# Channel attention on one core: in its second pass the first packed group is unfolded only behind the raw rows and the first streamed rows

## The chip, the cores and the metric

The kernel runs on one core of one Trainium2 chip. The metric is the device time in microseconds (us) of one execution. The kernel before took 721.81 us, the median of three runs (721.34 to 722.48).

## The reference, cut to what matters

```python
# x: (1, 384, 384, 384) bfloat16, w1d: (1,) bfloat16, k = 1
g = jnp.einsum("bhwc->bc", x) / (H * W)
s = _sigmoid(g * w1d[0])          # the loop over k has one turn, the padding is empty
return x * s[:, None, None, :]
```

Every channel is averaged over all 147456 pixels, and then the whole of x is multiplied by one factor per channel. The factor is known only when the last pixel has been read, so x is needed twice: once for the sum and once for the product. In bfloat16 x has 113.2 MB. The on-chip arena of the kernel holds 275 "rows"; a row is 384 values in each of the 128 partitions, 96 KB in all, and x is 1152 rows.

## The kernel before, in words

**Pass one** loads all 1152 rows with DMAs that SP issues (L236, `load`), and TensorE adds each row to one PSUM accumulator (L242 and L256, `sum_rows`). Of the rows, 785 are *streamed*: they pass through the arena and are lost, so that pass two has to load them again. The other 367 are *kept*, in two ways. The 71 *raw* rows lie in the arena as they are. The others are kept as *groups*, in packed form: a group of 4q rows is folded into 3q rows by bit operations on VectorE (L276 `bits`, L282 `join`), since the bits of a quarter of the rows fit into unused bits of the other three quarters; ScalarE keeps a note of whether they did (L313). There are ten groups: group 0 (16 rows), groups 1 to 8 (32 rows each, four in each of two columns of the arena) and group 9 (24 rows, whose packed rows wait in PSUM banks). At the end of pass one ScalarE makes the factor (L443, a sigmoid).

**Pass two** multiplies all 1152 rows and stores them (`scale`, L456, nearly always on VectorE; `store`, L466, by SP), and loads the 785 streamed rows again into whatever rows of the arena have become free. A group is turned back into rows by `unfold`: for each of its two pieces (16 rows each) come the steps `fields` (four `bits` and two `join`), `three` (one `bits`, one `join`, a `scale` of 12 rows) and `fourth` (one `bits`, a `scale` of 4 rows). A group needs scratch rows (the 8 rows called Y), and its column needs 8 rows (U or V) that hold raw rows at first; `needed` says when these have been stored.

**What sets the order.** Nothing in pass two is ordered on the chip by choice. A planner in the kernel's Python code runs ahead of time with a clock of its own, `now`, in steps of 0.05 us, which begins at 0 when the factor is ready. It assumes a time for every step (`TS`, `TT`), for every row that a DMA moves (`ROW` 0.2267 us) and for the landing of a DMA, and writes the instructions into the queue of each engine in the order in which they come in this plan. On the chip each engine takes its queue strictly in order, and waits where its next instruction needs something that is not there (class `Flow`). SP's queue holds all loads and stores of pass two: a store that waits for VectorE holds back every load behind it. These rules of the planner matter here:

- When VectorE is free in the plan, the planner takes the next step of a group already begun; if there is none, it may begin a group (`start_group`), but only if nothing is left of three pieces that GpSimd scales at the start (`alongside`), and if either the DMA backlog is at least 24 us or no landed rows wait (`landed`).
- Landed rows are scaled first as long as the backlog of DMA work is under 24 us; else unfolding comes first.
- Streamed rows are loaded into the longest run of free rows, at once if the run is 32 rows or more, else only if the backlog has fallen under 9 us (8 rows or more) or under 4 us (any number).

The rows in which the work begins: the raw rows are stored first, in pieces of 4, 4, 4, 4, 8, 8, 13 and 13 rows by VectorE, and 4, 4 and 5 by GpSimd. Arena rows 220 to 232 and 233 to 245 are the two 13-row pieces, 246 to 258 the three pieces of GpSimd, 259 to 266 the piece called T. The first streamed loads of pass two go into these rows. In the plan of the kernel before, the first group (group 7) begins at 13.00, when the last 13-row piece has been scaled and the first streamed rows have not landed.

Of the kernel before, what the change touches and what calls it, by code (L numbers as in the profile page):

```python
# [127 lines left out]
def kernel(  # L128
# [45 lines left out]
    BANKED = len(GROUPS)  # L174
# [30 lines left out]
    def rows(lo, n):  # L205
        return [("a", r) for r in range(lo, lo + n)]
# [168 lines left out]
    def of_group(g):  # L375
        return [i for i, piece in enumerate(pieces) if piece[0] == g]
# [93 lines left out]
    def unfold(k, first):  # L470

        g, lo, p = pieces[k]
        a, at = first + 3 * lo, first + 3 * GROUPS[g][1] + lo
        w, wc = flat(a, 3 * p), [rows(a + j * p, p) for j in range(3)]
        w0, w1, w2 = (flat(a + j * p, p) for j in range(3))
        ba, ca = Y, Y + PIECE
        u, b, c = flat(at, p), flat(ba, p), flat(ca, p)
        uc, bc, cc = rows(at, p), rows(ba, p), rows(ca, p)

        def fields():  # L480
            bits(u, w0, SHR, 4, AND, 0x0780, wc[0], uc)
            bits(b, w1, SHR, 8, AND, 0x0078, wc[1], bc)
            bits(c, w2, SHR, 12, AND, 0x0007, wc[2], cc)
            join(u, u, b, OR, uc + bc, uc)
            bits(b, w2, SHL, 4, AND, 0x8000, wc[2], bc)
            join(u, u, c, OR, uc + cc, uc)

        def three():
            wall = wc[0] + wc[1] + wc[2]
            bits(w, w, AND, 0x87FF, OR, 0x3800, wall, wall)  # L490
            join(u, u, b, OR, uc + bc, uc)
            scale(a, 3 * p)

        def fourth():

            bits(u, u, XOR, FIX, AND, 0xFFFF, uc, uc)
            scale(at, p)

        return [
            (fields, 4 * TS(p) + 2 * TT(p)),  # L500
            (three, TS(3 * p) + TT(p) + TT(3 * p)),
            (fourth, TS(p) + TT(p)),
        ]
# [66 lines left out]
    now = dve_at = 0.0  # L570
# [5 lines left out]
    def release(a, n):  # L576
        for i in range(a, a + n):
            idle[i] = True
# [14 lines left out]
    def send(chunk, a, lo, hi, then, known=None):  # L593

        waiting.append((dve_at, hi - lo, then, chunk, a, lo, [] if known is None else known))
# [11 lines left out]
    needed = [set(SCRATCH + rows(U, 8)), set(SCRATCH + rows(V, 8)), set(SCRATCH)]  # L607
# [31 lines left out]
    free = [True, True, True]  # L639
# [3 lines left out]
    bank_at = None  # L643
# [4 lines left out]
    def start_group():  # L648

        if not line:  # L650
            return False
        g = line[0]
        column = home[g]
        if needed[column] or not free[column] or g == BANKED and (bank_at is None or now < bank_at[1]):
            return False
        line.popleft()
        free[column] = False
        a, q = GROUPS[g]
        if g == BANKED:
            a = bank_at[0]  # L660

        below = 0
        if column < 2 and g != COLUMNS[column][0]:
            below = GROUPS[COLUMNS[column][COLUMNS[column].index(g) - 1]][1]

        def part():
            release(a + below, sent - below)

        def done():
            nonlocal out_rows  # L670
            out_rows += 1
            free[column] = True
            release(a + max(below, sent), 4 * q - max(below, sent))

        for k in of_group(g):
            fields, three, fourth = unfold(k, a)
            turns.extend((fields + (None,), three + (None,), fourth + (None,)))
        sent = 0
        if len(line) >= total - N_SPLIT and q == PAIR:

            f, t, _ = turns[-5]
            sent = 3 * PIECE
            turns[-5] = (f, t, lambda: send(KEPT, a, c_group[g], c_group[g] + sent, part, written))
        f, t, _ = turns[-1]
        turns[-1] = (f, t, lambda: send(KEPT, a + sent, c_group[g] + sent, c_group[g] + 4 * q, done, written))
        return True

    while True:

        if dve_at <= now:  # L690
            ahead = backlog()
            can = bool(turns)
            if not can and not alongside and (ahead >= PENDING or not landed):
                can = start_group()
            if landed and (ahead < PENDING or not can):
                chunk, a, lo, n, end = landed.popleft()
                scale(a, n, s=s_ps if alongside and now else s_bf)
                dve_at = now + TT(n)
                since = (a, lo) if since is None else since
                if end or ahead < MERGE:  # L700
                    b, first = since
                    send(chunk, b, first, lo + n, stored(b, lo + n - first))
                    since = None
            elif can:
                f, t, then = turns.popleft()
                f()
                dve_at = now + t
                if then:
                    then()
# [18 lines left out]
        if bank_at is None and len(line) <= total - BANKS_AT and got and max(got)[0] >= PS * 4 // 3:  # L728
# [7 lines left out]
            bank_at = (a, now + 5.0)  # L736
# [59 lines left out]
```

## Time and profile before

| what | value |
|---|---|
| time, median of three runs | 721.81 us (721.34 to 722.48) |
| profiled execution, first to last instruction (span) | 719.6 us |
| VectorE (DVE) busy | 494.0 us, 69% |
| TensorE (PE) busy | 210.5 us, 29% |
| ScalarE (ACT) busy | 115.7 us, 16% |
| bytes moved by DMA | 303.79 MB, mean 422 GB/s |
| HBM read, written | 190.41 MB, 113.25 MB |
| last matmul done, factor begun | 268.3 us |

The page gives no other time for the profiled execution than its span; the median of the runs lies 2.2 us above that. In the profile, L12 is line 12 of the kernel; DVE is VectorE, and SPq is the queue of SP, which issues the DMAs. A row of the timeline gives the start, the duration, the engine, the line, the operation, out<-in and a count; what stands in brackets is idle time and what ended it. 128x1536 is 128 partitions by 1536 elements, that is 4 rows of 384. A row of the windows gives a stretch of the span and the busy time of every engine in it, and at its end the granted TensorE clock, the busy share of the DMA engines and the rate that they moved.

### The profile page before, as it was taken

What the parts mean: (1) busy time and instruction counts of PE and PEld (TensorE: products, weight loads), DVE (VectorE), ACT (ScalarE), POOL (GpSimd) and SP (SyncE); (2) the same over time, 40 slices, a digit from 0 to 9 for tenths busy, and PEclk for the clock granted to TensorE, in tenths of its full rate; (3) what the DMA queues carried; (4) which work ended last, traced back from release to release, by engine and by line L of the source; (5) the groups of instructions that cost most, each with busy time, mean ns of one, the idle gap of its engine ahead of it and who ended that gap; (6) DMA issues with size and microseconds to landing.
All of it is one profiled execution on the core that took longest, in us unless ns stands there. A gap on an engine that the chain in (4) does not pass through costs nothing.

```text
span 719.6 us, 2061 instructions
## 1 busy us (share of the span) xinstructions
PE 210.5 (29%) x1202; PEld 0.3 (0%) x3; DVE 494.0 (69%) x471; ACT 115.7 (16%) x93; POOL 10.6 (1%) x7
## 2 busy tenths in 40 slices
PE   4678689888887770000000000000000000000000
PEld 0000000000000000000000000000000000000000
DVE  4600004887999819988999998999998985095500
ACT  3600003665777610002000000000000000000000
POOL 0000000000000005000000000000000000000000
PEclk9999999999999995555555555555555555555555
DMA  9999999999999979999999999999999999999997
GB/s 381 431 441 428 426 430 432 438 434 429 422 427 427 429 324 369 422 394 423 429 432 437 426 431 445 427 428 439 432 427 442 427 436 430 437 435 426 437 438 318
DMA packets 20173, 303.79 MB, mean 422 GB/s; under 512 B 2242, under 2 KB 2242, under 8 KB 6082
## 3 DMA queue, kind: packets, MB, share of 16 engines
q1 hardware_dynamic: 20160, 303.67, 99.0%
q8 instruction: 4, 0.07, 0.0%
q14 instruction: 7, 0.06, 0.0%
q10 hardware_dynamic: 2, 0.00, 0.0%
HBM read 190.41 MB, written 113.25 MB: 422 GB/s over the span
## 4 chain that ended last, share of the span: by engine, by line
DMA 61%; DVE 21%; ACT 6%; PE 5%; another core or an unknown queue 1%; SPq 0%; issue 0%; DVEq 0%
DMA arena<-in_x_dram 40%; DMA out_dram<-arena 21%; DVE arena L456 14%; ACT arena L313 6%; PE bank L242 5%; DVE arena L276 5%; DVE arena L282 2%; SPq L236 0%; ACT s_bf L443 0%; SPq L791 0%; DVEq L112 0%; SPq L106 0%
## 5 line engine op out<-in xcount | busy, mean ns | idle before, releaser
L456 DVE TENSOR_TENSOR arena<-arena,s_bf 128x4608 bf16<-128x4608 bf16 (+8 forms) x97 | 228.8, 2390 | 68.2 <-DMA arena<-in_x_dram 52.3
L276 DVE TENSOR_SCALAR arena<-arena 128x1536 uint16<-128x1536 uint16 (+2 forms) x247 | 145.3, 633 | 111.8 <-DMA arena<-in_x_dram 102.0
L242 PE MATMUL bank<-arena,ones 128*128 128x384 bf16 x1151 | 202.1, 336 | 48.9 <-DMA arena<-in_x_dram 48.9
L313 ACT ACTIVATE arena<-arena 128x3072 uint16<-128x3072 uint16 (+1 forms) x38 | 102.4, 2696 | 142.3 <-DVE arena L276 142.3
L282 DVE TENSOR_TENSOR arena<-arena 128x1536 uint16<-128x1536 uint16 (+2 forms) x114 | 121.0, 1061 | 5.2 <-PE bank L242 2.7
L529 PE MATMUL bank<-odd,ones 128*128 128x1 bf16 x1 | 0.2, 188 | 322.7 <-DVE odd L524 322.7
L456 POOL TENSOR_TENSOR arena<-arena,s_bf 128x1536 bf16<-128x1536 bf16 (+1 forms) x3 | 10.4, 3484 | 268.9 <-ACT bank L447 268.9
L386 ACT COPY arena<-bank 128x512 uint32<-128x512 uint32 (+1 forms) x7 | 4.0, 571 | 58.4 <-DMA out_dram<-arena 58.2
L456 DVE TENSOR_TENSOR arena<-arena,bank 128x1536 bf16<-128x1536 bf16 (+2 forms) x7 | 11.3, 1688 | 0.0
L242 PE MATMUL bank<-zeros,ones 128*128 128x384 bf16 x48 | 8.3, 326 | 0.0
L313 ACT ACTIVATION_READ_ACCUMULATOR arena<-arena 128x1 f32 x38 | 7.1, 186 | 0.0
L386 ACT COPY bank<-arena 128x512 uint32<-128x512 uint32 (+1 forms) x7 | 3.6, 566 | 0.0
L443 ACT ACTIVATE s_bf<-bank,w_sc 128x384 bf16<-128x384 f32 x1 | 0.6, 581 | 14.5 <-PE bank L242 14.5
L256 PE MATMUL bank<-arena,ones 128*128 128x384 bf16 x1 | 0.5, 478 | 6.9 <-DMA arena<-in_x_dram 6.9
L764 ACT ACT_TABLE_LOAD x1 | 1.3, 1283 | 0.7 <-PEq L780 0.7
L343 DVE TENSOR_SCALAR w_sc<-bank 128x1 f32<-128x1 f32 x1 | 0.2, 159 | 1.1 <-PE bank L338 1.1
L333 DVE MEMSET ones<- 128x128 bf16 x1 | 0.2, 165 | 1.0 <-SPq L106 1.0
L338 PE MATMUL bank<-w_bf,ones 1*128 1x1 bf16 x1 | 0.2, 181 | 2.1 <-DMA w_bf<-in_w1d_dram 2.1
L529 PEld LDWEIGHTS bank<-odd,ones 128*128 128x128 bf16 x1 | 0.1, 106 | 581.7 <-DVE odd L524 581.7
L533 DVE CAST odd_i<-bank 128x1 int32<-128x1 f32 x1 | 0.2, 159 | 0.3 <-PE bank L529 0.3
L447 ACT COPY bank<-s_bf 128x192 uint32<-128x192 uint32 x1 | 0.3, 323 | 0.0
L519 DVE TENSOR_REDUCE worst<-seen 128x1 f32<-128x38 f32 x1 | 0.2, 184 | 0.0
(8 smaller groups left out, 0.9 us busy)
## 6 DMA issues: line engine op xcount, KB each, us to landing
arena<-in_x_dram SPq DMA_DIRECT2D x15, 4608.0 KB, 35.4
arena<-in_x_dram SPq DMA_DIRECT2D x21, 1248.0 KB, 13.5
out_dram<-arena SPq DMA_DIRECT2D x7, 3072.0 KB, 33.1
arena<-in_x_dram SPq DMA_DIRECT2D x6, 3072.0 KB, 26.5
out_dram<-arena SPq DMA_DIRECT2D x4, 4608.0 KB, 39.2
arena<-in_x_dram SPq DMA_DIRECT2D x6, 2304.0 KB, 18.2
arena<-in_x_dram SPq DMA_DIRECT2D x3, 4512.0 KB, 27.0
out_dram<-arena SPq DMA_DIRECT2D x10, 1248.0 KB, 12.0
```

The source lines that it names most:

```text
L242: return pe.add_instruction(mybir.InstMatmult(name=nc.get_next_instruction_name(), ins=[pe.lower_ap(rhs), pe.lower_ap(ones[:])], outs=[pe. ...
L256: return nc.tensor.matmul(acc, lhsT=ones[:], rhs=arena[:, i, :], start=first, stop=last)
L276: lambda: nc.vector.tensor_scalar(out=dst, in0=src, scalar1=s0, scalar2=s1, op0=op0, op1=op1),
L282: "DVE", lambda: nc.vector.tensor_tensor(out=dst, in0=a, in1=b, op=op), reads=reads, writes=writes
L313: lambda: nc.scalar.activation(out=y, in_=y, func=ACTF.Copy, accum_out=seen[:, 2 * k + i : 2 * k + i + 1]),
L333: fl.add("DVE", lambda: nc.vector.memset(ones[:], 1.0), writes=["ones"])
L386: "ACT", lambda: nc.scalar.copy(dst.bitcast(u32), src.bitcast(u32)), reads=reads, writes=writes
L443: lambda: nc.scalar.activation(out=s_bf[:], in_=acc, func=ACTF.Sigmoid, scale=w_sc[:, 0:1]),
L447: "ACT", lambda: nc.scalar.copy(s_ps.bitcast(u32), s_bf[:].bitcast(u32)), reads=["s_bf"], writes=["bank0"]
L456: lambda: vec.tensor_tensor(out=v, in0=v, in1=s[:, None, :].to_broadcast([P, n, C]), op=Op.mult),
L529: lambda: nc.tensor.matmul(votes, lhsT=ones[:], rhs=odd[:], start=True, stop=True),
L764: nc.scalar.preload_act_table(ACTF.Sigmoid)
```

## The change

One condition is added where a group may begin:

```diff
     def start_group():
         if not line:
             return False
         g = line[0]
         column = home[g]
-        if needed[column] or not free[column] or g == BANKED and (bank_at is None or now < bank_at[1]):
+        if now < 26.0 or needed[column] or not free[column] or g == BANKED and (bank_at is None or now < bank_at[1]):
             return False
```

Until its clock shows 26.0 the planner begins no group. The rest of the planner is as it was, so everything behind this point of the plan comes out differently as a consequence: what VectorE does between 13 and 26, which rows are free when, how large the loads are that go into them, and where the stores stand in SP's queue.

What comes out, in the clock of the plan: the first group begins at 27.25 instead of 13.00, the second at 64.40 instead of 44.30, the third at 100.40 instead of 79.30, and the last at 327.55 instead of 315.90. Up to the 13-row load into arena row 220 the queue of SP is the same in both. From the last raw store on it reads (number of rows, and in brackets the arena row where they begin):

```
before                                  after
store 13 (233), load 8 (246)            store 13 (233), load 8 (246)
load 13 (220)                           load 13 (220)
store 12 of group 7                     store 8 (259)
load 13 (233)                           load 13 (233)
store 8 (259)                           store 8 (246)
store 8 (246)                           load 5 (254), load 8 (259)
store 13 (220)                          store 13 (220)
load 5 (254), load 8 (259)              load 8 (246)
load 8 (246), load 13 (220)             store 13 (233), store 5 (254)
store 13 (233), store 20 of group 7     load 13 (220)
store 5 (254)                           store 12 of group 7
```

In pass two SP issues 98 DMAs instead of 91: 35 loads instead of 32, and 63 stores instead of 59. They move the same 1937 rows (785 loads, 1152 stores). The instructions of pass one are the same.

## The prediction

> **What bounds the kernel now.** I read the page first, for the engine that is always busy:
>
> ```profile
> span 719.6 us, 2061 instructions
> ...
> PE 210.5 (29%) x1202; PEld 0.3 (0%) x3; DVE 494.0 (69%) x471; ACT 115.7 (16%) x93; POOL 10.6 (1%) x7
> ...
> DMA  9999999999999979999999999999999999999997
> ...
> q1 hardware_dynamic: 20160, 303.67, 99.0%
> ```
>
> The DMA engines are busy in every slice; SP's one queue fills them 99% of the span, while VectorE (DVE), the busiest engine beside them, works 69% of it. So the kernel moves 303.67 MB and little else counts. What can change the time is bytes (the same before and after), the rate, and stretches without traffic. Next I read the windows of pass two, which begins when the factor is made (268.33, a row further below):
>
> ```profile
> 264.00:268.00 4.00, 3.82 (x25) 0.00 (x0) 0.00 (x0) 0.00 (x0) 0.00 (x0) 1.00 0.42 171
> 268.00:271.00 3.00, 0.29 (x2) 0.00 (x0) 2.06 (x3) 0.90 (x2) 1.66 (x1) 0.99 0.08 31
> 271.00:282.00 11.00, 0.00 (x0) 0.00 (x0) 11.00 (x8) 0.00 (x0) 8.71 (x3) 0.50 1.03 422
> 282.00:288.00 6.00, 0.00 (x0) 0.00 (x0) 5.97 (x8) 0.00 (x0) 0.00 (x0) 0.50 1.02 332
> 288.00:312.00 24.00, 0.00 (x0) 0.00 (x0) 21.41 (x18) 0.00 (x0) 0.00 (x0) 0.50 1.01 419
> 312.00:318.00 6.00, 0.00 (x0) 0.00 (x0) 5.87 (x8) 0.00 (x0) 0.00 (x0) 0.50 0.98 331
> 318.00:348.00 30.00, 0.00 (x0) 0.00 (x0) 27.50 (x22) 4.00 (x7) 0.00 (x0) 0.50 1.01 427
> 348.00:378.00 30.00, 0.00 (x0) 0.00 (x0) 29.20 (x26) 0.00 (x0) 0.00 (x0) 0.50 1.01 429
> 378.00:450.00 72.00, 0.00 (x0) 0.00 (x0) 68.61 (x65) 0.00 (x0) 0.00 (x0) 0.50 1.01 434
> 450.00:600.00 150.00, 0.19 (x1) 0.11 (x1) 135.65 (x112) 0.00 (x0) 0.00 (x0) 0.50 1.00 433
> 600.00:712.00 112.00, 0.00 (x0) 0.00 (x0) 48.28 (x15) 0.00 (x0) 0.00 (x0) 0.50 1.00 432
> ```
>
> The last column is the rate in GB/s. Three things stand in it. Around 268 there is a hole (171 and 31), while the sum ends and the first row is scaled; both kernels have it, and their queues are the same there. Two patches, 282 to 288 and 312 to 318, run at 332 and 331 although the busy share beside them is about 1: the packets take longer, the engines are not idle. Against 430 each costs 6 x (1 - 332/430) = 1.4 us, 2.75 together. And the stretch of small transfers (318 to 378) runs at 427 and 429, the later one at 432 to 434.
>
> **What the change moves.** It adds no arithmetic and no bytes: the same rows are scaled, unfolded, loaded and stored. It postpones the unfolding of group 7, and the rest of the order follows. The timeline of the place, before (SPq rows are SP issuing):
>
> ```profile
> 268.33 0.58 ACT L443 ACTIVATE s_bf<-bank,w_sc 128x384 bf16<-128x384 f32 x1 [14.50 <-PE bank L242]
> ...
> 269.92 8.92 SPq L466 DMA_DIRECT2D out_dram<-arena  x9
> 278.88 0.54 SPq L236 DMA_DIRECT2D arena<-in_x_dram  x1
> 279.74 2.19 SPq L466 DMA_DIRECT2D out_dram<-arena  x2
> 281.07 1.49 DVE L276 TENSOR_SCALAR arena<-arena 128x1536 uint16<-128x1536 uint16 x3
> 282.02 3.05 SPq L236 DMA_DIRECT2D arena<-in_x_dram  x2
> ...
> 283.93 0.95 DVE L282 TENSOR_TENSOR arena<-arena 128x1536 uint16<-128x1536 uint16 x1
> 284.80 1.35 DVE L276 TENSOR_SCALAR arena<-arena 128x4608 uint16<-128x4608 uint16 x1
> 286.07 0.95 DVE L282 TENSOR_TENSOR arena<-arena 128x1536 uint16<-128x1536 uint16 x1
> 286.94 4.22 DVE L456 TENSOR_TENSOR arena<-arena,s_bf 128x4608 bf16<-128x4608 bf16 x2
> 289.51 0.34 SPq L466 DMA_DIRECT2D out_dram<-arena  x1
> ...
> 292.57 0.33 SPq L236 DMA_DIRECT2D arena<-in_x_dram  x1
> 292.94 8.43 SPq L466 DMA_DIRECT2D out_dram<-arena  x3
> ...
> 298.25 2.76 DVE L456 TENSOR_TENSOR arena<-arena,s_bf 128x4992 bf16<-128x4992 bf16 x1 [0.24 <-DMA arena<-in_x_dram]
> ```
>
> `fields` runs from 281.07 to about 284.8 (3.7 us), `three` from there to 289.5 (4.7 us), and releases the 12-row store at 289.51. After the change that store is gone from this place. SP's next entry is the store of the first 8 streamed rows, which waits for their load (issued at 278.88) and their scale. So **VectorE gets some 8 us of idle time, and a wait on a load takes the place of a wait on VectorE**. Behind the waiting store stand all later loads, the 13-row one into row 233 first. The question is whether the traffic already issued lasts until SP goes on. I call that the cover.
>
> The durations that I use:
>
> ```profile
> arena<-in_x_dram SPq DMA_DIRECT2D x21, 1248.0 KB, 13.5
> ...
> arena<-in_x_dram SPq DMA_DIRECT2D x11, 768.0 KB, 11.4
> ```
>
> 13 rows are 1248 KB = 1.278 MB, at 428 GB/s 3.0 us; 8 rows 1.84 us, 5 rows 1.15, 12 rows 2.75. From issue to landing they take 13.5 and 11.4 (median), so most of that is the queue ahead of them. On VectorE a scale of 13 rows takes 2.76 (the row at 298.25), and one of 8 rows I put at 1.75 (2.76 x 8/13 = 1.70).
>
> Step by step, after the change:
> - Everything up to the load of 13 rows into row 220, the last of the two issued from 282.02 on, is in both orders. It lands at 298.2 (the row at 298.25 waited for it).
> - Store of 8 (row 259): its load, from 278.88, lands by the median at 290.3; plus 1.75 it is issued near 292.0. Cover: 298.2 - 292.0 = 6.2 us. Before, the 12-row store at this place came at 289.51, with 8.7.
> - Load of 13 (233): waits for the same raw store as the row at 292.57 did. No change. Cover after it: 298.2 + 1.84 + 3.0 = 303.0.
> - Store of 8 (246): its load, issued near 282.5, lands by the median near 293.9, plus 1.75 = 295.7. Cover 7.3.
> - Load of 5, then load of 8 (259), which waits until the first 8-row store has landed, 298.2 + 1.84 = 300.0. Cover then 303.0 + 1.84 + 1.15 = 306.0, less 300.0: 6.0 us.
> - Store of 13 (220): VectorE does `fields` first (295.7 to 299.4), then the scale, to 302.2. Cover 307.8 - 302.2 = 5.6.
> - Load of 8 (246): waits for the second 8-row store, 304.9. Cover 310.8 - 304.9 = 5.9. Store of 13 (233): near 305.0, cover 7.6.
>
> So the cover never falls under **5.6 us** in the thin part. Needed is the time from issue to the first byte: the first store of pass two is issued at 269.92, and the rate goes from 31 up to 271 to 422 behind it, so that is about 1.1 us, between nothing and 2. The spare is 4.5 us. The removed wait costs and gives nothing, because VectorE's work there was hidden under traffic before, and the idle time that replaces it is hidden too. If the cover were gone, each us that SP is late would be a us of the end.
>
> **What is late next.** The groups come 12 to 21 us later in the plan, and with them the free runs of 24 rows and more. So the stretch of small transfers lasts longer: before, the first 24-row load is at 356.3, the first row below; in the plan it moves by 27 us (87.45 to 114.85).
>
> ```profile
> 356.32 5.15 SPq L236 DMA_DIRECT2D arena<-in_x_dram  x2
> ```
>
> Such a stretch costs the difference of rates: 27 us x (1 - 428/433) = **0.3 us**, which is also the price of 98 DMAs instead of 91 (7 more). From below this term is 0 (429 against 432), from above 27 x (1 - 419/434) = 0.9, with the row of 288 to 312. VectorE has the slack for the later groups: 48.28 us busy of 112 in the last stretch. At the end before, the last three scales are done while the queue is long:
>
> ```profile
> 671.95 9.69 DVE L456 TENSOR_TENSOR arena<-arena,s_bf 128x6144 bf16<-128x6144 bf16 x3 [8.00 <-DMA arena<-in_x_dram]
> ```
>
> They end at 681.7, and the span at 719.6: 36 us of stores are still queued there. After, the last entries are loads of 48, 44 and 9 rows and stores of 32, 48, 44 and 9. When the 44-row load lands, 10 us behind the 48-row one whose scales take 9.9, the load of 9 and the stores of 32 and 48 are still to move, 89 rows x 0.23 = 20 us; VectorE needs 9.1 us for 44 rows (9.69 for the 47 in the row). Cover some 11 us: thinner, but there.
>
> One rule of the Trainium skill speaks against the change. DMA: Bandwidth & Descriptors, section "Anatomy of one DMA — SWDGE (gpsimd) path", gives a DMA about 2.0 us fixed on top of its bytes; were that in series, seven more would be 14 us, though its fit is for DMAs of GpSimd. The trace does not agree that it is in series: with it 13 rows would move at 1.278 MB / 5.0 us = 256 GB/s, and the rows of 318 to 378 have 427 and 429.
>
> **The sum.** 719.6 + 0.0 (wait exchanged) + 0.3 (small transfers) = 719.9 us of span; what lies around the span is 2.2 us (median 721.81 against 719.6). That gives 722.1.
>
> **The rivals.**
> 1. *The thin queue makes more slow patches: slower.* The patch at 282 came right after the thinnest time of all: the 13-row raw store was issued at 278.5 and landed in 6.2 us, 3.2 of them for the traffic ahead of it. If thin cover is what slows the packets, then five covers in a row of about 6 us, from 292 to 305, lie just where it may decide, and the longer stretch of small transfers gives another chance later. It decides from a cover of some 6 us. Price: two patches of 1.4 us, plus 0.3: 724.9. For it: both patches lie in the first 50 us of pass two, with small transfers, and none later. Against: the stretch from 318 to 378 has small transfers and no patch.
>
> ```profile
> 278.51 6.21 DMA out_dram<-arena
> ```
>
> 2. *The patches go: faster.* Both lie on `fields` steps of VectorE (the row at 281.07; the next below). After, `fields` stands elsewhere. If VectorE's bit operations beside those very transfers were the cause, 2.75 us go and 0.3 comes: 719.4. If only the second goes, because the first belongs to transfers that stay, 720.7, which is not to be told from no change. Against: the third `fields`, at 292.53, lies in a stretch of 419.
>
> ```profile
> 292.53 1.49 DVE L276 TENSOR_SCALAR arena<-arena 128x1536 uint16<-128x1536 uint16 x3
> ...
> 313.17 1.49 DVE L276 TENSOR_SCALAR arena<-arena 128x1536 uint16<-128x1536 uint16 x3
> ```
>
> 3. *A fixed time for every DMA, in series.* Seven more at the 2.7 us that pass from the factor at 268.3 to the full rate at 271: 19 us, 741. The rows of 318 to 378 exclude most of it.
> 4. *The change does nothing.* It would if the plan came out the same. The order of the instructions of the two kernels differs, so there is no chance in it.
>
> **How the numbers follow.** A measurement of this kernel can tell 0.2%, 1.4 us, from no change. The forecast (queue never dry, patches about as many) has 0.52 with 720.4 to 723.2 as its own range, the case of one patch less included. Rival 1 has 0.30, rival 3 0.02, rival 2 with both patches gone 0.16. So faster 0.16, same 0.52, slower 0.32. The range reaches to both rivals: from 719.4 (both patches gone) to 725.2 (two patches more, with most of the upper bound of the small transfers: 721.8 + 2.8 + 0.6). What is left out is the part of rival 1 with three patches or more, rival 3, and a gain beyond the patches.
>
> **What would show it.** In the changed kernel's windows the rate from 290 to 310 should be 415 or more, with no slice of 3 us under 380 that is not a patch with a busy share near 1; a low busy share there would mean a dry queue and prove the covers wrong. VectorE should be idle some 8 us between 281 and 296, waiting on loads. The stretch of small transfers should last until about 380. The span should be 719 to 721. Wrong would be the forecast if the sum of the patches changed by more than one of 1.4 us, or if a wait of SP ended in a window without traffic.

## The result, and the profile after

The changed kernel takes 722.98 us (median of 18 runs, 720.83 to 725.57), the kernel before 721.36 in the runs beside it (median of 18, 720.36 to 722.78). The ratio is 1.002, with a 95% interval of 1.0012 to 1.0029: the change costs some 1.5 us (0.9 to 2.1). That is more than nothing, and the interval lies on both sides of the 0.2% that the prediction gives as the least that can be told from no change. The forecast was 722.1 with 0.3 us for the change.

The page of the changed kernel, the lines that answer to those of before:

```profile
span 721.6 us, 2070 instructions
...
PE 214.5 (30%) x1202; PEld 0.3 (0%) x3; DVE 494.8 (69%) x473; ACT 115.7 (16%) x93; POOL 10.6 (1%) x7
...
DMA  9999999999999979999999999999999999999996
...
q1 hardware_dynamic: 21168, 303.67, 98.9%
```

Same bytes, the same work on VectorE, and a queue that fills the DMA engines 98.9% of a span that is 2.0 us longer (before: 99.0% of 719.6). The only digit of the DMA row that differs is the last: 6 instead of 7. The loss is thus not an engine or a wait in the middle; one has to look at the rate and at the end. First the place of the change, in the timeline (SPq rows are SP issuing; the bracket is idle time and what ended it):

```profile
281.88 3.08 SPq L236 DMA_DIRECT2D arena<-in_x_dram  x2
288.42 1.76 DVE L456 TENSOR_TENSOR arena<-arena,s_bf 128x3072 bf16<-128x3072 bf16 x1 [7.41 <-DMA arena<-in_x_dram]
290.21 0.34 SPq L466 DMA_DIRECT2D out_dram<-arena  x1
292.62 0.33 SPq L236 DMA_DIRECT2D arena<-in_x_dram  x1
294.43 1.76 DVE L456 TENSOR_TENSOR arena<-arena,s_bf 128x3072 bf16<-128x3072 bf16 x1 [4.25 <-DMA arena<-in_x_dram]
...
296.22 0.34 SPq L466 DMA_DIRECT2D out_dram<-arena  x1
296.61 3.70 SPq L236 DMA_DIRECT2D arena<-in_x_dram  x2
...
302.62 0.34 SPq L466 DMA_DIRECT2D out_dram<-arena  x1
...
304.87 0.33 SPq L236 DMA_DIRECT2D arena<-in_x_dram  x1
305.73 1.73 SPq L466 DMA_DIRECT2D out_dram<-arena  x2
```

VectorE now waits twice for a load, 7.41 and 4.25 us, where `fields` and `three` stood. SP's stores and loads follow in the order that the plan wrote. Then the rate, in the windows of pass two (last three columns: granted TensorE clock, busy share of the DMA engines, GB/s):

```profile
282.00:288.00 6.00, 0.00 (x0) 0.00 (x0) 0.00 (x0) 0.00 (x0) 0.00 (x0) 0.50 0.98 338
288.00:306.00 18.00, 0.00 (x0) 0.00 (x0) 12.71 (x11) 0.00 (x0) 0.00 (x0) 0.50 1.02 422
306.00:312.00 6.00, 0.00 (x0) 0.00 (x0) 6.00 (x5) 0.00 (x0) 0.00 (x0) 0.50 1.00 375
312.00:318.00 6.00, 0.00 (x0) 0.00 (x0) 5.93 (x8) 0.00 (x0) 0.00 (x0) 0.50 1.01 426
318.00:366.00 48.00, 0.00 (x0) 0.00 (x0) 45.71 (x37) 3.99 (x7) 0.00 (x0) 0.50 1.01 428
369.00:375.00 6.00, 0.00 (x0) 0.00 (x0) 5.97 (x7) 0.00 (x0) 0.00 (x0) 0.50 0.99 339
375.00:426.00 51.00, 0.00 (x0) 0.00 (x0) 48.33 (x42) 0.00 (x0) 0.00 (x0) 0.50 1.01 432
426.00:432.00 6.00, 0.00 (x0) 0.00 (x0) 4.78 (x8) 0.00 (x0) 0.00 (x0) 0.50 0.98 391
450.00:600.00 150.00, 0.00 (x0) 0.00 (x0) 143.11 (x128) 0.00 (x0) 0.00 (x0) 0.50 1.01 434
600.00:712.00 112.00, 0.18 (x1) 0.10 (x1) 52.03 (x22) 0.00 (x0) 0.00 (x0) 0.50 1.01 434
```

The busy share stays at 0.98 to 1.02, so the queue never ran dry. The patch at 312 to 318 is gone (426), the one at 282 is as it was, and three others have come, at 306, 369 and 426. The kernel before has there:

```profile
306.00:312.00 6.00, 0.00 (x0) 0.00 (x0) 3.71 (x3) 0.00 (x0) 0.00 (x0) 0.50 1.01 416
369.00:375.00 6.00, 0.00 (x0) 0.00 (x0) 5.30 (x3) 0.00 (x0) 0.00 (x0) 0.50 0.98 420
426.00:432.00 6.00, 0.00 (x0) 0.00 (x0) 5.93 (x10) 0.00 (x0) 0.00 (x0) 0.50 0.99 423
```

Counted against 430 as the prediction did (6 x (1 - rate/430)), the four patches cost 1.28 + 0.77 + 1.27 + 0.54 = 3.9 us, against 2.75 before; from 450 on the changed kernel is slightly quicker (434 and 434, against 433 and 432). Last, the end of the queue, before and after:

```profile
716.00:718.00 2.00, 0.00 (x0) 0.00 (x0) 0.00 (x0) 0.00 (x0) 0.00 (x0) 0.50 0.14 58
718.00:720.00 2.00, 0.00 (x0) 0.00 (x0) 0.00 (x0) 0.00 (x0) 0.00 (x0) 0.50 0.00 0
```

```profile
716.00:718.00 2.00, 0.00 (x0) 0.00 (x0) 0.00 (x0) 0.00 (x0) 0.00 (x0) 0.50 0.28 120
718.00:720.00 2.00, 0.00 (x0) 0.00 (x0) 0.00 (x0) 0.00 (x0) 0.00 (x0) 0.50 0.12 48
```

In both kernels most of the 16 DMA engines have stopped by then, and a few are still writing; after the change they write some 2 us longer. The trace records 16 landings for every DMA, one for each engine, and these say how many. The last stores, as microseconds behind the mean of the 16:

```
before        last store, mean 716.09   -1.0 -1.0 -0.9 -0.8 -0.7 -0.7 -0.5 -0.4 -0.2 -0.2 -0.1  0.2  1.4  1.5  1.6  1.7
before_again  last store, mean 716.52   -1.4 -1.3 -1.3 -0.9 -0.7 -0.5 -0.3 -0.3 -0.2  0.0  0.1  1.2  1.3  1.4  1.5  1.5
after         last store, mean 716.80   -1.4 -1.3 -1.3 -1.3 -1.3 -1.2 -1.2 -1.2 -0.9 -0.4  0.7  1.0  1.3  2.4  3.0  3.2
after         48-row store, mean 704.76 -1.4 -1.3 -1.3 -1.3 -1.3 -1.2 -1.2 -1.1 -0.9 -0.4  0.6  1.0  1.3  2.4  3.0  3.2
after_again   last store, mean 716.66   -1.2 -1.2 -1.2 -1.1 -1.1 -1.1 -0.9 -0.8 -0.5 -0.5 -0.2  0.2  1.3  2.5  2.9  2.9
```

This is the reading that the prediction did not make. After the change three engines end 2.4 to 3.2 us behind the mean; before, the last end 1.5 to 1.7 behind it. The 48-row store shows the same distances 12 us earlier, so they are carried along from store to store: an engine that is late stays late by the same time, as if no other took work from it. I call the distance from the mean to the last engine the **lag**. The span ends with the lag, and so two numbers describe a kernel here: the mean of the last landings (all bytes at the mean rate) and the lag.

The packets of the trace say what the lag is made of. They carry no engine's name, but a packet begins within some ns of the end of the one before it on its engine, and each of SP's DMAs has nine records on every engine (eight packets of data and a last one of 4 B), so every engine can be followed through pass two. Its slow time is what its packets took beyond the median for their size. From 270 us on, engines in the order in which they end, in us:

```
before     end behind the mean  -1.0 -0.9 -0.9 -0.8 -0.7 -0.7 -0.5 -0.4 -0.3 -0.2 -0.0  0.2  1.4  1.5  1.6  1.7
           slow time             2.1  2.4  2.1  2.4  2.7  2.6  3.0  3.0  3.1  3.2  3.1  2.9  1.5  4.6  4.9  4.8
after      end behind the mean  -1.4 -1.3 -1.3 -1.3 -1.3 -1.3 -1.2 -1.1 -0.9 -0.4  0.6  1.0  1.3  2.4  3.0  3.2
           slow time             2.6  2.3  2.5  2.6  2.6  2.6  2.4  2.8  2.8  2.8  3.9  4.9  5.2  5.7  7.0  6.2
after_asc  end behind the mean  -1.1 -1.1 -1.1 -1.0 -1.0 -1.0 -0.9 -0.8 -0.8 -0.8 -0.4  0.7  1.1  1.2  3.4  3.6
           slow time             1.4  1.5  1.5  1.4  1.6  1.5  1.7  1.6  1.8  1.6  1.9  3.3  3.3  3.7  5.1  5.4
```

(after_asc is one of the experiments below.) The slow time and the short pauses between packets together give the end of every engine to 0.1 us; the one large pause is 3.2 us, on the engine of before that has 1.5. In after_again and split34, with the order of after, the last two engines have 6.4 to 6.8 us of slow time and the first ten 2.5 to 3.3. **So the lag is slow packets that fall on a few engines.** A window shows their mean over the 16 engines, the end of the kernel the engine that had most of them.

### The profile page after: what moved, and what is told of

The parts are those of the page before. It is cut to its first block, busy times and chain, and to the rows that moved or that the text cites. A ratio compares the mean times of both kernels' runs of the same rounds, so it can differ in the third digit from the quotient of the medians.

```text
span 721.6 us, 2070 instructions
## 1 busy us (share of the span) xinstructions
PE 214.5 (30%) x1202; PEld 0.3 (0%) x3; DVE 494.8 (69%) x473; ACT 115.7 (16%) x93; POOL 10.6 (1%) x7
## 3 DMA queue, kind: packets, MB, share of 16 engines
q1 hardware_dynamic: 21168, 303.67, 98.9%
## 4 chain that ended last, share of the span: by engine, by line
DMA 60%; DVE 25%; ACT 5%; PE 5%; issue 0%; SPq 0%; another core or an unknown queue 0%; DVEq 0%
DMA arena<-in_x_dram 39%; DMA out_dram<-arena 21%; DVE arena L456 15%; DVE arena L276 7%; ACT arena L313 5%; PE bank L242 5%; DVE arena L282 4%; SPq L236 0%; ACT s_bf L443 0%; DVEq L112 0%; SPq L791 0%; SPq L106 0%
## 5 line engine op out<-in xcount | busy, mean ns | idle before, releaser
L456 DVE TENSOR_TENSOR arena<-arena,s_bf 128x4608 bf16<-128x4608 bf16 (+9 forms) x99 | 229.4, 2346 | 82.0 <-DMA arena<-in_x_dram 66.1
L242 PE MATMUL bank<-arena,ones 128*128 128x384 bf16 x1151 | 206.1, 340 | 45.0 <-DMA arena<-in_x_dram 44.8
L256 PE MATMUL bank<-arena,ones 128*128 128x384 bf16 x1 | 0.5, 479 | 6.7 <-DMA arena<-in_x_dram 6.7
```

The source lines that it names most:

```text
L242: return pe.add_instruction(mybir.InstMatmult(name=nc.get_next_instruction_name(), ins=[pe.lower_ap(rhs), pe.lower_ap(ones[:])], outs=[pe. ...
L256: return nc.tensor.matmul(acc, lhsT=ones[:], rhs=arena[:, i, :], start=first, stop=last)
L456: lambda: vec.tensor_tensor(out=v, in0=v, in1=s[:, None, :].to_broadcast([P, n, C]), op=Op.mult),
```

## The experiments

Each was run on the kernel before or after with one edit. The ratio is that to the kernel before, with its 95% interval in brackets. The patches are worked out from windows of 6 us as above, for the places where each profile has them; mean and lag from the 16 landings of the last store. One profile is one execution, whose time scatters by about 1 us, so mean, lag and span of a single row carry little; groups of rows do. The spans of the profiles are near those of the other executions: the median is 719.9 for 35 executions of the kernel before and 721.2 for the 18 of the changed one. The two kernels with a held store further down (hold7, hold12) have means of 716.4 and 719.0 and lags of 2.2 and 2.1.

| kernel | edit on | DMAs in pass two | patches, us | mean | lag | span | ratio |
|---|---|---|---|---|---|---|---|
| before | | 91 | 2.75 | 716.1 | 1.7 | 719.6 | |
| before_again | | 91 | 3.1 | 716.5 | 1.5 | 719.8 | |
| before_asc | before | 91 | 2.9 | 716.4 | 2.0 | 720.2 | 0.9998 [0.9988, 1.0008] |
| after | | 98 | 3.9 | 716.8 | 3.2 | 721.6 | 1.0020 [1.0012, 1.0029] |
| after_again | | 98 | 3.2 | 716.7 | 2.9 | 721.2 | |
| after_asc | after | 98 | 1.7 | 715.5 | 3.6 | 720.7 | 1.0018 [1.0009, 1.0026] |
| split34 | after | 99 | 3.0 | 716.8 | 3.0 | 721.5 | 1.0022 [1.0013, 1.0031] |
| split16 | before | 122 | 3.1 | 717.9 | 2.2 | 721.7 | 1.0011 [1.0002, 1.0020] |
| begin14 | before | 88 | 2.9 | 716.1 | 2.8 | 720.8 | 1.0000 [0.9990, 1.0010] |
| begin22 | before | 90 | 1.5 | 714.9 | 2.7 | 719.4 | 1.0004 [0.9996, 1.0013] |
| thick6 | before | 93 | 1.3 | 715.7 | 4.8 | 722.2 | 1.0009 [0.9996, 1.0022] |
| thick8 | before | 98 | 1.9 | 715.9 | 3.3 | 720.9 | 1.0013 [1.0004, 1.0023] |

**My theory at this point** was that of the forecast with more patches: the thin queue slows packets (the prediction's rival 1). The rivals were a price for every DMA, addresses, and the lateness of the groups.

### The two kernels again (after_again, before_again)

No edit; is what the profiles differ in a property of the kernel or of one execution?

> The changed kernel unchanged, profiled a second time. Its first profile had stretches of lowered rate at 282 to 285 (267 GB/s), 306 to 312 (386 and 364) and 369 to 375 (343 and 335), and its last transfers tapered off from 715 to 719.6. If these patches come from the order of the DMAs, they stand at the same places again, within 1 us, and cost the same 1.3, 0.6 and 1.1 us; if they are chance, they stand elsewhere. The taper at the end is a property of the order if it again takes over 4 us, chance if it takes 2.5 to 3 as in the kernel before.

> The kernel before unchanged, profiled a second time, with patches at 282 to 286 and 312 to 318 the first time. Order theory: the same two places, about 1.4 us each, and full rate at 306 to 311 and 369 to 375. Chance theory: other places or another number of patches. The taper at the end took some 3 us the first time.

```profile
282.00:288.00 6.00, 0.00 (x0) 0.00 (x0) 0.00 (x0) 0.00 (x0) 0.00 (x0) 0.50 0.97 333
306.00:312.00 6.00, 0.00 (x0) 0.00 (x0) 6.00 (x5) 0.00 (x0) 0.00 (x0) 0.50 1.01 394
369.00:375.00 6.00, 0.00 (x0) 0.00 (x0) 5.97 (x7) 0.00 (x0) 0.00 (x0) 0.50 1.00 364
426.00:432.00 6.00, 0.00 (x0) 0.00 (x0) 5.05 (x9) 0.00 (x0) 0.00 (x0) 0.50 0.97 401
```

Those are windows of after_again; before_again has its own two:

```profile
282.00:288.00 6.00, 0.00 (x0) 0.00 (x0) 5.97 (x7) 0.00 (x0) 0.00 (x0) 0.50 0.97 324
...
312.00:318.00 6.00, 0.00 (x0) 0.00 (x0) 5.97 (x8) 0.00 (x0) 0.00 (x0) 0.50 0.97 314
```

Every patch comes again at its place in a second execution, so the places belong to the kernel and not to one run. Their sizes vary: 3.2 us in after_again, 3.1 in before_again, so that the 1.1 us by which the patches differed between the first two profiles is nearly gone, while the lag is again 2.9 against 1.5.

### How much queued traffic is enough (hold7, hold12)

On the kernel before, one store is held back by 7 or 12 copies of a PSUM bank onto itself on ScalarE, which was idle, so that the traffic ahead of it shrinks. The order of all queues stays; the copies are added work.

```diff
+    def hold(a, m):
+        half = banks[0][:, 0:BANK].bitcast(u32)
+        s = fl.writer[("a", a)]
+        for _ in range(m):
+            s = fl.add("ACT", lambda: nc.scalar.copy(half, half),
+                reads=[("bank", 0)], writes=[("bank", 0)], after=[s])
+        return [s]
...
-            known.append(store(chunk, a, lo, lo + n))
+            held = hold(a, 12) if chunk == STREAMED and lo == 662 else ()
+            known.append(store(chunk, a, lo, lo + n, held))
```

> The kernel before, with one store of 13 rows (issued at 354.8, with 9 us of issued traffic ahead of it) held back some 4.3 us by seven ScalarE copies of a PSUM bank onto itself; no bytes and no VectorE step are changed. The issued traffic falls to some 5 us at this one place, where the profile of before runs at 426 to 437 GB/s. Theory of the thin queue: a patch of 1 to 1.4 us between 356 and 372 though the DMA engines never run dry. Rival (only a dry queue costs, the forecast's working): 425 or more all through, and the time within 0.3 us of before.

> As the run before, with twelve copies, some 7.3 us: the issued traffic falls to about 2 us. Thin queue: a patch of 1.4 us or more between 357 and 372. Rival: since 1.1 us are enough from issue to the first byte, still 425 or more and the time within 0.3 us of before. If the busy share falls under 0.9 with no slow packets, the queue did run dry, and the rival's working of the cover is what was wrong.

In the trace the held store was issued at 359.01 in hold7, with traffic ahead that landed up to 364.12, and at 361.66 in hold12, with traffic up to 363.74: covers of 5.1 and 2.1 us. The windows of hold7:

```profile
357.00:366.00 9.00, 0.00 (x0) 0.00 (x0) 8.93 (x10) 1.89 (x4) 0.00 (x0) 0.50 1.02 427
...
372.00:378.00 6.00, 0.00 (x0) 0.00 (x0) 5.03 (x2) 0.00 (x0) 0.00 (x0) 0.50 1.01 409
```

and of hold12:

```profile
360.00:363.00 3.00, 0.00 (x0) 0.00 (x0) 2.97 (x6) 1.57 (x3) 0.00 (x0) 0.50 0.69 290
363.00:366.00 3.00, 0.00 (x0) 0.00 (x0) 3.00 (x3) 0.00 (x0) 0.00 (x0) 0.50 1.05 356
...
372.00:378.00 6.00, 0.00 (x0) 0.00 (x0) 5.03 (x2) 0.00 (x0) 0.00 (x0) 0.50 0.97 352
```

With 5 us the thin queue costs 9 x (1 - 427/430) + 6 x (1 - 409/430) = 0.4 us. With 2 us the share falls to 0.69, and the price is 3 x (1 - 290/430) + 3 x (1 - 356/430) + 6 x (1 - 352/430) = 2.6 us; the single times are 722.18 and 724.90 (before_again 721.84, after_again 723.19, the kernel before beside them 723.50). Single runs of the kernel before differ by as much, so the price is read from the windows.

The packets of hold12 show what went wrong there. Nine of the 16 engines stood still when SP issued the held store at 361.66, the first four or more from 360.6 on, and the packets that end this stand begin at 362.49, 0.8 us behind the issue. So the 1.1 us that the prediction needed from issue to first byte were not too small. What was too large is the cover, which it counted to the last landing: the traffic ahead landed between 360.70 and 363.74, so that the first engine was done 3.0 us before the last. In hold7 the traffic ahead landed from 360.77 to 364.12, 1.8 us of cover for the first engine, and no engine stood still. In the changed kernel the least cover to the last landing is 5.3 us (at 302.62 and at 364.67), and to the first landing 2.2 and 1.7: still more than 0.8.

### Never thin, and does it help (thick6, thick8)

On the kernel before, the planner may load any number of rows when its backlog falls under 6 or 8 us instead of 4, so SP issues earlier and the queue stays long.

```diff
-    BIG, CAP, PART, LOW, LAST = 32, 48, 16, 9.0, 4.0
+    BIG, CAP, PART, LOW, LAST = 32, 48, 16, 9.0, 6.0
```

> The kernel before with one number of the planner changed: rows of any number are loaded again once the backlog of the plan has fallen under 6 us instead of 4. In the order that comes out (93 DMAs in pass two, before 91) no DMA behind the first raw stores is issued with fewer than about 30 rows still on their way; before has moments with 21 and 26. Theory of the thin queue: the patch at 312 to 318 goes, no other comes, and the time falls by about 1.0 us (0.9986) if the 16 engines end as close together as in before (2.7 to 3.4 us). Rival (patches are not due to the thin queue): a patch of 1 us or more somewhere between 290 and 400. If the patch goes and the time does not fall, the lag of the last engines decides.

> The same with 8 us: again no thin moment, and 98 DMAs, as many as in the changed kernel. If the loss of the changed kernel is the number of its DMAs, this one loses as much, +1.4 us (1.002). If the number costs 0.03 us each, as in the run with the cut stores, +0.2 us, and the patch that goes gives 1.2 back: about -1.0 us. Its own lag of the last engines moves that by half a microsecond either way.

Windows of thick6, and behind them one of thick8:

```profile
327.00:333.00 6.00, 0.00 (x0) 0.00 (x0) 5.64 (x9) 2.92 (x5) 0.00 (x0) 0.50 1.01 375
...
333.00:366.00 33.00, 0.00 (x0) 0.00 (x0) 29.42 (x27) 1.06 (x2) 0.00 (x0) 0.50 1.01 429
```

```profile
327.00:336.00 9.00, 0.00 (x0) 0.00 (x0) 8.97 (x9) 0.00 (x0) 0.00 (x0) 0.50 1.01 371
```

Counted as before, there are patches of 0.8 and 1.2 us at 327, and the loads with the slow packets there (13 rows issued at 318.7, 17 rows at 321.8) had 46 and 49 rows ahead of them, some 11 us. **So a thin queue is not needed for a patch, and rival 1 is not the whole mechanism.** Something remains of it: over ten profiles, DMAs of pass two issued with 20 to 29 rows ahead had 0.31 us of slow time for each engine in the mean (45 cases), those with 30 or more 0.01; that is a correlation, and thick6 and thick8 are its exceptions. Nor did a longer queue pay: 1.0009 and 1.0013, with the mean of the landings early (715.7 and 715.9) and lags of 4.8 and 3.3.

### What a DMA costs (split16)

On the kernel before, every store of more than 16 rows is issued in parts of at most 16: 31 DMAs more, the same bytes and order.

```diff
-            known.append(store(chunk, a, lo, lo + n))
+            for e, f in split(n, 16):
+                known.append(store(chunk, a + e, lo + e, lo + f))
```

> The kernel before, with every store of more than 16 rows cut into stores of at most 16 that follow each other at once in SP's queue: 31 more DMAs in pass two, nothing else moved, and nearly all of them where much traffic is queued. It prices a DMA by itself. Theory that the number of DMAs is the small term of the sum (7 more for 0.3 us, so 0.04 to 0.06 us each): +1.2 to +1.9 us, a ratio of 1.0017 to 1.0026. Rival, a fixed time for every DMA in series (2 us or more): +62 us. If the number costs nothing at all: 1.000.

```profile
q1 hardware_dynamic: 24624, 303.67, 99.1%
...
out_dram<-arena SPq DMA_DIRECT2D x34, 1536.0 KB, 34.5
```

The time grows by 0.0011 x 722 = 0.8 us (0.1 to 1.4), which is 0.026 us for each DMA (0.005 to 0.047). The seven more of the change come to 0.2 us, 0.3 at most. Their number is not the loss; thick8, with 98 DMAs as well, has its mean at 715.9, earlier than before.

### Addresses (before_asc, after_asc)

The streamed rows are loaded in ascending instead of descending order, in both kernels; everything else is equal.

```diff
-                lo = N_STREAM - todo - n
+                lo = todo
```

> The kernel before, with one line changed: pass two takes the streamed rows in ascending instead of descending order, so every DMA has the same size, the same place in SP's queue and the same arena rows, and only the addresses in memory differ. The patches at 282 to 286 and 312 to 318 came back at the same places in a second profile. Theory of the thin queue and of aligned engines: the patch at 312 to 318 stays, and the spread of a DMA's 16 landings rises to about 2.7 us as before. Theory of the addresses: it goes or stands elsewhere, and the time moves by 0.5 to 1.5 us either way.

> The changed kernel with the same one line: ascending addresses, the order of its DMAs as it was. Its patches stood at 282 to 285, 306 to 312, 369 to 375 and near 428, twice. Thin queue: the ones at 306 and 369 stay, and it is again 1 to 2 us slower than the kernel before. Addresses: they go or move, and the difference to the ascending version of the kernel before shrinks to the price of 7 DMAs, 0.3 to 0.5 us, or turns round.

Windows of before_asc, then of after_asc:

```profile
282.00:288.00 6.00, 0.00 (x0) 0.00 (x0) 5.97 (x8) 0.00 (x0) 0.00 (x0) 0.50 1.00 335
...
312.00:318.00 6.00, 0.00 (x0) 0.00 (x0) 5.43 (x8) 0.00 (x0) 0.00 (x0) 0.50 0.99 317
```

```profile
306.00:312.00 6.00, 0.00 (x0) 0.00 (x0) 6.00 (x5) 0.00 (x0) 0.00 (x0) 0.50 1.01 424
369.00:375.00 6.00, 0.00 (x0) 0.00 (x0) 5.97 (x6) 0.00 (x0) 0.00 (x0) 0.50 1.00 408
426.00:432.00 6.00, 0.00 (x0) 0.00 (x0) 5.01 (x8) 0.00 (x0) 0.00 (x0) 0.50 1.00 419
```

With other addresses the patches of before stand as they were, so the addresses are not their cause. In the changed kernel the addresses may matter for the size: its three late patches nearly vanish (0.1, 0.3 and 0.2 us), though the loads of 8 and 13 rows at 304.6 and 365.9 have the same 26 rows ahead as in after (where they are issued at 304.9 and 366.7); this is one profile. The mean of after_asc is 715.5, ahead of every profile of before, and it is still slower by 1.0018. Its lag is 3.6. **A larger sum of patches is therefore not what makes the changed kernel slow:** by the table of the engines, after_asc has less slow time in the mean than before (2.4 us against 3.0), but two engines have 5.1 and 5.4 of it.

### Other beginnings for the groups (begin14, begin22)

The condition of the change with 14.0 and with 22.0 instead of 26.0. With 22.0 the first group begins at 22.0 in the plan's clock (before 13.00, after 27.25), the second at 55.05 (44.30, 64.40) and the last at 322.55 (315.90, 327.55).

```diff
-        if needed[column] or ...
+        if now < 22.0 or needed[column] or ...
```

> The changed kernel with the limit at 14 instead of 26 in the plan's clock: the first group begins a little later than before and sooner than after, and pass two has 88 DMAs (before 91, after 98). If what costs is the lateness of the first group, it is between the two, +0.1 to +0.5 us. If what costs is the number of DMAs, it is 0.1 to 0.2 us faster than before. If what costs is patches that hang on the particular order, it can land anywhere within 2 us, and its profile's patches and the spread of its last landings tell which way: +-1.0 us by each patch of 1.4 us and by each 2 us of spread at the end.

> The changed kernel with the limit at 22 of the plan's clock: the first group begins at 22.0, the second at 55.05 and the last at 322.55 (after the change 27.25, 64.40 and 327.55; before 13.00, 44.30 and 315.90), so nearly as late as after, but pass two has 90 DMAs (after 98, before 91). If lateness of the groups costs, about two thirds of the loss, 1.0013. If the loss is the DMAs and the lag of the last engines, the DMAs give nothing, and the ratio is 1.000 with a lag of the slowest engine behind the mean of the 16 near 1.7 us as in before, or 1.001 to 1.002 with a lag near 3.

Windows of begin22:

```profile
282.00:288.00 6.00, 0.00 (x0) 0.00 (x0) 0.14 (x1) 0.00 (x0) 0.00 (x0) 0.50 0.97 320
306.00:312.00 6.00, 0.00 (x0) 0.00 (x0) 5.24 (x7) 0.00 (x0) 0.00 (x0) 0.50 1.01 426
312.00:318.00 6.00, 0.00 (x0) 0.00 (x0) 4.95 (x5) 0.00 (x0) 0.00 (x0) 0.50 1.02 434
318.00:348.00 30.00, 0.00 (x0) 0.00 (x0) 29.64 (x28) 4.00 (x7) 0.00 (x0) 0.50 1.01 426
```

Begin22 delays the groups by more than half of what the change does (9.0 of 14.25 us for the first), and its time is not to be told from before: 1.0004 [0.9996, 1.0013]. That VectorE's work comes later is hardly the loss, though the 1.0013 that this theory gave is just the upper end of the interval. It has one patch instead of two, and its mean is 1.2 to 1.6 us earlier than before; its lag of 2.7 takes most of this back. Begin14 has one patch at 306 to 312 (300 GB/s) instead of 312 to 318, and no difference in time. Its lag of 2.8 with a ratio of 1.0000 shows how little one profile's lag is worth by itself.

### One load in two parts (split34)

In the profiles of after the spread of a DMA's 16 landings (last minus first) grows from 3.4 us at 376 to 4.6 at 432 (after_again and after_asc have 4.5 there) and stays above 4 to the end; before keeps 2.7 from 345 on. The traffic there holds a load of 34 rows (issued at 410.4, landed at 432.0), a size that before does not have. Here it is issued as two of 17.

```diff
-                load(STREAMED, a, lo, lo + n)
+                for e, f in ((0, 17), (17, 34)) if n == 34 else ((0, n),):
+                    load(STREAMED, a + e, lo + e, lo + f)
```

> The changed kernel with its one load of 34 rows issued as two loads of 17 behind each other; nothing else moves. In all three profiles of this order the spread of a DMA's 16 landings rises from 3.4 to 4.5 us while this load and the 24-row load behind it are moved (426 to 434), and it stays to the end. If the shape of this load is the cause, the spread stays at 3.4 and the time falls by about 1 us against the changed kernel, to a ratio of 1.0005 to before. If the place in the order is, the jump is there again, and the ratio is 1.002.

The time stays at 1.0022, and the spread again jumps there, from 3.8 to 4.4 us. The shape of this load is not the cause. The engines followed through after show the jump itself: between 420 and 436 the six engines that end last lose 0.7 to 1.4 us each to slow packets, nine of the others nothing, so the mean moves by 0.4 us and the lag goes from 2.4 to 3.3.

No version tried is quicker than the kernel before.

## Why the prediction was right, and where it fell short

- **What bounds the kernel** holds: the share of the queue, the bytes and VectorE's busy time are as before.
- **The wait exchanged at no cost** holds. The issue times worked out by hand were 292.0, 292.6, 295.7, 300.0, 302.2, 304.9 and 305.0; the timeline has 290.21, 292.62, 296.22, 299.98 (the second load of the row at 296.61), 302.62, 304.87 and 305.73. The windows from 288 to 306 run at 422 with a share of 1.02. VectorE's idle time is 7.41 + 4.25 = 11.7 us; "some 8 us" was the work that went, while the step's own times (from 281.07 to 290.3, and from 292.0 to 293.9) give 11.1. It cost nothing, as said.
- **The spare** was too large: 5.6 us of cover less 1.1 needed gave 4.5. The need was about right (0.8 us in hold12), but the cover was counted to the last landing, and the first engine runs dry some 3 us earlier. Counted to the first landing, the least cover is 1.7 us and the spare 0.9. The conclusion stands with less room.
- **Small transfers, 0.3 us**: the first 24-row load is the second of the two issued from 380.10 on (383.3), 27 us later than before as worked out, and split16 gives 0.2 us for seven DMAs. (The bound from below was put at 0, but the same sum with 429 against 432 gives 0.2.)

```profile
380.10 3.54 SPq L236 DMA_DIRECT2D arena<-in_x_dram  x2
```

- **The end**: the cover of VectorE's last scales was right, as no window up to 712 falls under 434. **The step that fell short is the sum itself**: it added the change of the rate to the old span and so took the end of the 16 engines as it was. Over the four profiles of the changed order (after, after_again, after_asc, split34) the mean of the last landings is 716.45, over the three of the old order (before, before_again, before_asc) 716.33: 0.1 us later, as good as forecast. The lags are 3.2 and 1.7 in the mean: 1.4 us more. Together 1.5, as timed. So the missing term is the lag, and it was sized at nothing. That the measured time lies in the range all the same is luck in this part: the range had room for patches, and the lag used it.
- **The signs** were met in part: the span came out at 721.6 and 721.2 instead of 719 to 721, and the rate from 290 to 310 at 410 instead of 415 or more, because the patch at 306 reaches into it. The sum of the patches changed by 1.1 us, inside the 1.4 that were allowed.
- **Rival 2** (`fields` makes the patches) falls: in 282 to 288 of after VectorE is busy 0.00 and the rate is 338. **Rival 3** falls to 0.026 us for a DMA. The rule of the Trainium skill that was weighed there (DMA: Bandwidth & Descriptors, "Anatomy of one DMA — SWDGE (gpsimd) path", about 2.0 us fixed) would give 62 us for split16 if the fixed time were in series; the 0.8 us timed say that behind a full queue of SP it is not. **Rival 1** had the right sign and twice the size (3.1 us against 1.5): patches did come anew, but after_asc is as slow without most of them. Slow packets are the loss, not by their sum as rival 1 had it, but by how unevenly they fall on the engines.

What stays open is why. Runs with one edit excluded as the cause of the loss the number of DMAs, the addresses and the shape of the 34-row load, and made the lateness of the groups unlikely; a thin queue is not necessary for slow packets, but it goes with them too often to be dropped. They did not show what makes the packets of certain loads slow, nor why in this order some of them, as between 420 and 436, fall on the engines that are late already.

## What to carry to other kernels

In a kernel that is bound by DMA, the time is the end of the latest of the 16 engines, so read the last landings of each engine beside the mean rate: here the mean moved 0.1 us and the lag 1.4. The lags in these profiles go from 1.5 to 4.8 us with the same bytes, and a forecast should carry that as a term with bounds instead of taking the old end over. Idle time that is put on a hidden engine cost nothing here; count the cover to the landing of the first engine and not of the last (they were 3 us apart), and compare it with the time from issue to first packet (0.8 us).

## What was not expected of the hardware

- The engines' landings of one DMA lie 0.2 us apart right behind the hole at 268, when the queue has been dry, and 2.2 (before) and 2.3 us (after) apart at 286.5. From 436 on the spread changes little: 2.7 in before, 4.6 in after, though in thick6 it still grows from 5.4 to 6.1. In hold12 it fell to 0.3 to 0.7 when the queue ran dry at 360 to 366, and was back at 2.9 by 564. No other engine takes work from a late one.
- The patches at full busy share come again at the same places when the same kernel is run again, and one at 282 comes in every kernel tried (320 to 354 GB/s, and weaker with 394 and 399 in thick6 and thick8), with other addresses, and with VectorE idle or busy beside it.
- A DMA that was issued while engines stood still began on them 0.8 us behind its issue (361.66 to 362.49 in hold12), and the first store of pass two 0.9 us behind its own (269.92 to 270.78).
- One more DMA behind a full queue costs 0.026 us (0.005 to 0.047) in stores of at most 1.5 MB.
